# Scores' product with the keys' low parts over all 128 rows

## The chip, the cores and the metric

The kernel is one program on 1 core of one Trainium2 chip. The metric is the device time of one execution in microseconds (us). It is timed in several runs, and the median counts. Beside these runs stands one profiled execution, from which all rows below come. Line numbers with an L are those of the kernel before, unless the text says that they are of the changed kernel.

## The reference, cut to what matters

The whole computation has three stages: a recurrence over 768 tokens (4 batches, 8 heads), a feed-forward with a convolution, and an attention of four experts. The change is in the third:

```
for e in range(4):
    q = x @ wq[e]; k = x @ wk[e]; v = x @ wv[e]        # x: 4 x 768 x 320, heads of 64
    scores = (q @ k.T) / 8                             # causal
    a = softmax(scores)
    out += (gate of e, if e is among a token's best two) * (a @ v @ wo[e])
```

The inputs are float32, and the factor of 200 on `wq` and `wk` makes the scores large, so that the products are made from two parts of each operand: a high part in fp32r (what TensorE takes in one pass) and the rest, the low part, also in fp32r.

## The kernel before, in words

The recurrence and the feed-forward run side by side through the first 655 us. Then `setup_c` opens the tiles of the attention in the memory that the recurrence leaves, loads its weights through staging tiles `ws` (L637, tag "A", 6 buffers) and splits each into high and low part (L468 on ScalarE, L469 on VectorE). The last blocks of the feed-forward still run: their products are L551 and L574, their gates pass ScalarE at L468 (`gh`), L584 and L588, VectorE at L586, GpSimd at L469 (`gl`) and L589. From about 710 us only the attention is left.

`proj` makes queries, keys, values and gates of half of a batch. An expert has 64 dimensions, so that two experts share the 128 rows of a product. The tile `q` has, for expert e of a pair, the high parts of the queries in the 64 rows `Z[e]` and the low parts in the other 64. The tile `k` has the keys' high parts in both halves. The low parts of the keys stand in `kl`, two experts of a pair in one slot: expert 0 in rows 0 to 63, expert 1 in rows 64 to 127.

`weigh` then makes the scores of a block of 128 queries and one expert, for nk = 128 to 768 keys, in pieces (cuts) of at most 512 columns of PSUM. Each piece has two products: L748 multiplies all 128 rows of `q` with `k` (high and low queries times high keys), and L749 adds the high queries times the low keys, with the 64 rows of that expert alone. After the last piece of a block L751 adds the causal mask, in bf16. VectorE takes the maximum (L753), ScalarE the exponential (L755, into a tile `A`), GpSimd the scaling (L770), TensorE the transposes (L784), ScalarE and VectorE copy them (L789, L787), and TensorE weighs the values (L800) and multiplies with the output weights (L817). Copies of the result go through a tile `y` (L819, 2 buffers) to memory (L820). While the feed-forward still runs, tiles `A` come from the same 6 buffers as `ws`; afterwards from a larger pool.

Every matrix product in the program is a pair of instructions, a load of the stationary operand (PEld) and the product that streams the moving one (PE). The order on each engine is made by a scheduler when the program is built, from the code's order and from when it takes buffers to be free; on the chip each engine works its list in order.

Of the kernel before, what the change touches and what calls it, by code (L numbers as in the profile page):

```python
# [22 lines left out]
# the upper bits of the float64 that is float32's least normal, as a float32  # L23
# [7 lines left out]
def merge(streams, end=1e9):  # L31
    """Runs generators side by side: each yields how far along it is, and the one least far along goes on."""
    live = [[-9.0, k, g] for k, g in enumerate(streams)]
    while live:
        m = min(live)
        if m[0] > end:
            return
        try:
            m[0] = next(m[2])
        except StopIteration:  # L40
            live.remove(m)


def paced(g, start, span):
    """The progress that a generator yields as a share of its own, in the common time."""
    for f in g:
        yield start + span * f


class Kernel:  # L50
    """Heads of a tile are (b, hq, al, be), head = 4 hq + 2 al + be of batch b; a tile n holds 64
    tokens, two chunks of 32, of all batches. Columns of the tiles are u = (p, c), p = (b, hq)."""
# [4 lines left out]
    # ---------------------------------------------------------------- recurrence  # L57
    def setup_a(self, ctx):
        tc, nc = self.tc, self.nc
        cp = self.cp = ctx.enter_context(tc.tile_pool(name="acst", bufs=1))  # L60
        self.wk = ctx.enter_context(tc.tile_pool(name="awk", bufs=2))
        self.w = cp.tile([128, 32, 32], F32, name="w")
        self.kb = cp.tile([128, 16, 2, 2, 32], F32, name="kb")
        # rows of a head's a, then of the products of its tokens' a and k; beside them its state and values
        self.a = [cp.tile([128, 2, 2, 16, 32], F32, name=f"a{j}") for j in range(2)]
        self.SV = cp.tile([128, 2, 2, NP, 40], F32, name="SV")
        self.ra = cp.tile([128, NP, 2, 2, 32], F32, name="ra")
        # of each be the rows of its k and b and, in the other half, of its state; beside them what they are weighed with
        self.LB = [cp.tile([128, 2, NP, 2, 40], F32, name=f"LB{j}") for j in range(2)]
        self.RB = cp.tile([128, 2, NP, 2, 32], F32, name="RB")  # L70
        self.P = [cp.tile([128, 32, 32], F32, name=f"P{j}") for j in range(3)]
        # rows (p % 2, be, t)
        self.U = [cp.tile([128, NP // 2, 104], F32, name=f"U{j}") for j in range(2)]
        self.VZ = cp.tile([128, NP, 2, 2, 40], F32, name="VZ")
        self.VT = cp.tile([128, NP, 2, 64], F32, name="VT")
        self.sT = [cp.tile([128, NP, 104], F32, name=f"sT{j}") for j in range(2)]
        self.S = [cp.tile([128, NP, 2, 40], F32, name=f"S{j}") for j in range(2)]
        self.g21 = cp.tile([128, 8, 2, 16], F32, name="g21")
        self.d1 = cp.tile([128, 8, 32], F32, name="d1")
        self.M1 = cp.tile([128, 8, 2, 16], F32, name="M1")  # L80
        self.po = self.ps[3][:, 1].rearrange("p (a b) -> p a b", a=2)
        nc.vector.memset(self.w[32:64], 1.0)
        nc.gpsimd.memset(self.kb[32:64], 0.0)
        nc.gpsimd.memset(self.a[0][32:64], 0.0)
        nc.vector.memset(self.P[0][:, :, 0:1], 1.0)
        nc.vector.memset(self.po[:, 1], 0.0)
        nc.vector.memset(self.ps[1][:, 1, 256:], 0.0)
        cst = cp.tile([128, 164], F32, name="cst")
        self.ident, self.mask = cst[:, :128], cst[:, 128:160]
        self.m0, self.m1, self.m2 = cst[:, 160:161], cst[:, 161:162], cst[:, 162:163]  # L90
        self.cst = cst
        self.t = {}
        self.work = self.nn = 0
# [8 lines left out]
    def consts_b(self):  # L102
        """As consts_a(), what the first tile's preparation doesn't need."""
# [18 lines left out]
    def load_a(self, n):  # L122
        """Of each pair of heads side by side in the rows, the one's and the other's."""
# [9 lines left out]
    def load_v(self, k):  # L133
        """The values of a chunk, at the places that they are read from."""
# [10 lines left out]
    def load_ra(self, k):  # L145
        """Of each pair of heads side by side in the rows, the columns of one and of the other."""
# [13 lines left out]
    def mm(self, ns, *a, **k):  # L160
        """A product beside which the feed-forward runs, with what it takes of the tensor engine."""
# [7 lines left out]
    def prep(self, n):  # L169
# [4 lines left out]
        def early(tag, shape, name):  # L174
            """The second tile's come before the first one is done, and take room of the feed-forward."""
# [5 lines left out]
        for k in range(1, 5):  # L181
            x = early("xd", [128, 32, 16], "L1") if k == 1 else wk.tile([128, 32, 32 >> k], F32, name=f"L{k}", bufs=1)
            # not amid the solve of the tile before, that more waits for
# [30 lines left out]
        # of each head the products of the tokens' a with their k and with their b  # L214
# [20 lines left out]
        # the two halves' blocks of I + G, one to a lane (q, half, u), and the block below them  # L235
# [5 lines left out]
        # the first tile's solve goes before the weights' conversion: it holds the tiles of the latter  # L241
# [10 lines left out]
        # rows (half, t) of the blocks below, of heads u of the one half and u + 8 of the other  # L252
# [47 lines left out]
        # the blocks below, of two heads at a time, times those above their right; then times those above their left  # L300
# [98 lines left out]
    def post(self, k):  # L399
# [12 lines left out]
        def po(p0):  # L412
            """While there is no feed-forward the second half takes a bank of its."""
# [43 lines left out]
    # ---------------------------------------------------------------- convolved feed-forward  # L457
# [13 lines left out]
    def narrow(self, name, src, n):  # L471
        """float32 of a block of float64 weights, put together from their bits; magnitudes under
        float32's least normal give zero."""
# [33 lines left out]
    def ff(self):  # L507
        """The feed-forward of all tiles; the second product of a step of two blocks runs beside the
        first one of the next step."""
# [90 lines left out]
        k = 0  # L600
# [17 lines left out]
    # ---------------------------------------------------------------- expert attention  # L618
    def setup_c(self, ctx):
# [14 lines left out]
        for dst, nm, n, rows in ((self.wvg, "w_vg", 260, 3), (self.wqk, "w_qk", 512, 3), (self.wo, "w_o", DM, 2)):  # L634
            for k in range(rows):
                s = cw.tile([128, S], F32, tag="A", name="ws", bufs=6)[:, :n]
                nc.sync.dma_start(s, i[nm][k])  # L637
                self.split(dst[:, k, 0], dst[:, k, 1], s)
        self.c = [{} for _ in range(B)]
        self.lone = False  # L640
        self.apool, self.nA, self.nT = cw, 6, 2
        self.turns = dict.fromkeys("stmo", 0)

    def bank(self, kind):
        """Scores, transposes, the other products, the values' sums: each in turn in its banks of PSUM;
        there are fewer while the feed-forward still runs."""
# [10 lines left out]
    def proj(self, b, h):  # L657
        """Queries, keys, values and gates of half of a batch's tokens."""
# [5 lines left out]
        if h == 0:  # L664
            t["k"] = cw.tile([128, 4, S], F32R, name="k", bufs=2)
            t["kl"] = cw.tile([128, 2, S], F32R, name="kl", bufs=2)
# [6 lines left out]
        # high and low parts of rows 0..127, 128..255, and of the last 64 together  # L673
# [19 lines left out]
        # queries of an expert: the one half of the rows has the high, the other the low part; keys: both the high  # L693
        for m, z in ((0, 0), (2, 1), (1, 2), (3, 3)):
# [4 lines left out]
            for e in range(2):  # L699
                r, o = Z[e], Z[1 - e]  # L700
                hi, lo = (q[:, 2 * m + e], q[o, 2 * m + e]) if m < 2 else (k[:, 2 * m - 4 + e, cs], kl[r, m - 2, cs])
                if m < 2:
                    # the queries take the scores' scale, a power of two
# [29 lines left out]
    def weigh(self, b, i, pr):  # L733
        """The weighted attention of a block of queries, of a pair of experts."""
# [6 lines left out]
        for e in range(2):  # L741
            r = slice(64 * e, 64 * e + 64)
# [3 lines left out]
            for c0, c1 in zip(cuts, cuts[1:]):  # L746
                ce = 2 * pr + e
                nc.tensor.matmul(sp[:, c0:c1], q[:, ce, 128 * j:128 * j + 128], k[:, ce, c0:c1], start=True, stop=False)  # L748
                nc.tensor.matmul(sp[:, c0:c1], q[r, ce, 128 * j:128 * j + 128], kl[r, pr, c0:c1], start=False,  # L749
# [10 lines left out]
    def scale(self, b, i, pr):  # L760
        """The weights over their sums and times the gates."""
# [11 lines left out]
    def turn(self, b, i, pr):  # L773
        """The transposes of the weights."""
# [18 lines left out]
    def values(self, b, i, pr):  # L793
        """The values' sums by these weights."""
# [15 lines left out]
    def result(self, b, i, pr):  # L810
        """The product with the experts' output weights."""
        nc, cw = self.nc, self.cwk
        if pr:
# [4 lines left out]
            y = cw.tile([128, DM], F32, name="y")  # L818
# [4 lines left out]
    # ---------------------------------------------------------------- all of it  # L823
    def run(self):
        tc, nc = self.tc, self.nc
        with ExitStack() as top:
            self.dp = top.enter_context(tc.tile_pool(name="dram", bufs=1, space=DRAM))
            self.x2 = self.dp.tile([B, S, DM], F32, name="x2")
            # pairs of banks: recurrence; second product; first product, preparation; transposes, results
# [52 lines left out]
    def merge(self, streams, side):  # L882
        """Runs the streams by progress, and as much of the one beside them as the work of the tensor engine calls for."""
# [17 lines left out]
    def attention(self, ff, top, bctx):  # L901
        """The blocks of queries one after the other, the weights of the next beside the values of the
        last, the projections before they are needed, and the rest of the feed-forward at first."""
# [40 lines left out]
def layouts(inputs):  # L944
    """The inputs as the tiles read them: permuted, repeated or with rows left out, no arithmetic."""
# [3 lines left out]
    # axes of heads(): b hq al be n c t e  # L949
# [10 lines left out]
    def bits(x):  # L960
        """float64 as its raw bits; float32 as it is."""
        return x.view(np.int64) if x.dtype == np.float64 else x

    # rows of w_in: (al, hq, be, e < 32), then (hq, be, al, e >= 32) twice
# [45 lines left out]
```

## Time and profile before

| what | value |
|---|---|
| runs | 1004.41, 997.58 and 1007.2 us, median 1004.41 |
| profiled execution | span 1001.0 us from first to last instruction, 31990 instructions |
| PE / PEld busy | 814.1 us (81%) / 678.6 us (68%) |
| DVE / ACT / POOL busy | 741.2 (74%) / 585.6 (59%) / 510.2 (51%) us |
| mean granted TensorE clock | 0.908 of full speed |

The span is 3.4 us under the median of the runs and inside their spread of 9.6 us; the profiled execution's own device time is not listed apart from its span. Busy shares are means over stages of different kind; which engine sets the time is read stage by stage in the rows further down. Times of matrix products include the filling and emptying of the array, so that neighbouring products overlap in the listing: how long one holds the engine is the distance from its start to the next start.

### The profile page before, as it was taken

The page shows a single profiled execution, that of the slowest core. Times are in us where ns is not written, and L with a number is a line of the kernel's source. Part 1 is how long each engine was busy: PE and PEld are TensorE (multiplying, and loading weights), DVE is VectorE, ACT ScalarE, POOL GpSimd, SP SyncE. Part 2 cuts the span into 40 slices and gives each one's busy share as a digit, 9 for nine tenths or more (in the row PEclk, how much of TensorE's full clock was granted, in tenths as well). Part 3 has the DMA queues.
Part 4 walks back from the last instruction along what each step waited for, and adds up shares of the span by engine and source line. Part 5 has one row for each costly group of instructions (what it writes and reads, how often), then busy time and mean ns, then how long its engine had stood idle before and what let it go on. Part 6 is the DMA issues. An engine that isn't in the chain of part 4 may idle for free.

```text
span 1001.0 us, 31990 instructions
## 1 busy us (share of the span) xinstructions
PE 814.1 (81%) x13112; PEld 678.6 (68%) x13112; DVE 741.2 (74%) x1675; ACT 585.6 (59%) x1379; POOL 510.2 (51%) x614
## 2 busy tenths in 40 slices
PE   1365649968797878787778789859999999999998
PEld 1255548757686767667677678848777767777766
DVE  6887995988979898979888985546565646666544
ACT  0164648747575656565557577747566555655554
POOL 6455665655647465655656565654234333233342
PEclk9995569978889789978898999879999999999999
DMA  5345553635363535444344445141110100010000
GB/s 115 95 139 133 138 121 85 149 81 114 75 142 90 123 77 122 117 100 102 93 97 121 96 101 121 43 117 32 35 33 21 34 14 28 28 34 14 16 12 34
DMA packets 143491, 81.20 MB, mean 81 GB/s; under 512 B 113858, under 2 KB 127042, under 8 KB 142386
## 3 DMA queue, kind: packets, MB, share of 16 engines
q1 hardware_dynamic: 138450, 74.34, 30.5%
q0 software_dynamic: 4896, 4.83, 2.2%
q8 instruction: 103, 1.69, 0.7%
q14 instruction: 42, 0.34, 0.1%
HBM read 51.63 MB, written 11.80 MB: 63 GB/s over the span
## 4 chain that ended last, share of the span: by engine, by line
PE 43%; DVE 28%; DMA 10%; ACT 9%; issue 5%; POOL 2%; SPq 2%; DVEq 0%; ACTq 0%; POOLq 0%
PE ps L163 6%; PE ps L800 5%; PE ps L749 5%; PE ps L697 4%; DVE cv L586 4%; PE ps L784 4%; PE ps L551 4%; PE ps L748 3%; PE ps L574 3%; DMA xd<-xs 3%; DVE t L261 3%; DVE Q L200 3%; DMA xs<-xe 3%; DVE a L211 3%; PE ps L817 3%
## 5 line engine op out<-in xcount | busy, mean ns | idle before, releaser
L770 POOL TENSOR_TENSOR A<-A,rs 128x128 f32<-128x128 f32 (+5 forms) x96 | 87.7, 934 | 145.0 <-DVE rs L768 81.0
L586 DVE SCALAR_TENSOR_TENSOR cv<-h,cw,cv 128x256 f32<-128x256 f32 (+1 forms) x192 | 103.4, 567 | 34.2 <-ACT cv L584 32.7
L574 PE MATMUL ps<-wout,gh 128*128 128x320 f32 x384 | 94.4, 343 | 12.6 <-ACT gh L468 12.3
L551 PE MATMUL ps<-xh,win 128*128 128x256 f32 x384 | 93.5, 301 | 11.7 <-ACT xh L527 10.7
L430 POOL TENSOR_TENSOR RB<-RB,cst 64x256 f32<-64x256 f32 x96 | 79.5, 828 | 32.3 <-ACT RB L429 18.4
L753 DVE TENSOR_REDUCE nm<-ps 128x1 f32<-128x128 f32 (+5 forms) x96 | 59.8, 623 | 46.9 <-PE ps L751 36.9
L755 ACT ACTIVATE A<-ps,nm 128x128 f32<-128x128 f32 (+5 forms) x96 | 60.8, 634 | 55.5 <-DVE nm L753 42.5
L551 PE MATMUL ps<-xl,win 128*128 128x256 f32 x384 | 92.6, 296 | 0.1
L589 POOL TENSOR_TENSOR cv<-cv,h 128x512 f32<-128x512 f32 (+1 forms) x48 | 62.2, 1297 | 59.6 <-ACT cv L588 58.8
L469 POOL TENSOR_TENSOR gl<-cv,gh 128x512 fp32r<-128x512 f32 x48 | 63.2, 1316 | 34.9 <-ACT gh L468 33.2
L551 PEld LDWEIGHTS ps<-xh,win 128*128 128x128 f32 x384 | 70.8, 202 | 14.4 <-ACT xh L527 11.6
L261 DVE TENSOR_TENSOR t<-TT,G 128x1 f32<-128x1 f32 (+4 forms) x180 | 77.0, 428 | 4.7
L574 PEld LDWEIGHTS ps<-wout,gh 128*128 128x128 f32 x384 | 68.3, 208 | 15.5 <-ACT gh L468 13.6
L551 PEld LDWEIGHTS ps<-xl,win 128*128 128x128 f32 x384 | 69.8, 199 | 0.9 <-POOL xl L529 0.2
L163 PE MATMUL ps<-RB,LB 104*40 104x32 f32 (+1 forms) x1536 | 49.9, 217 | 25.0 <-DVE xe L445 15.7
L163 PEld LDWEIGHTS ps<-RB,LB 104*40 104x40 f32 (+1 forms) x1536 | 43.2, 133 | 32.7 <-issue 18.8
L163 PE MATMUL ps<-kb,a 40*32 40x64 f32 x1536 | 37.5, 257 | 33.9 <-DVE kb L207 23.9
L163 PE MATMUL ps<-VZ,KB 128*40 128x80 f32 x768 | 47.1, 288 | 21.6 <-ACT VZ L359 21.4
L574 PE MATMUL ps<-wout,gl 128*128 128x320 f32 x192 | 61.0, 347 | 1.8 <-POOL gl L469 1.8
L800 PE MATMUL ps<-AT,v 128*64 128x128 f32 x672 | 57.4, 286 | 0.3 <-DVE mx L726 0.3
L749 PE MATMUL ps<-kl,q 64*128 64x256 f32 (+3 forms) x144 | 57.6, 400 | 0.0
L163 PEld LDWEIGHTS ps<-VZ,KB 128*40 128x40 f32 x768 | 40.2, 152 | 25.7 <-ACT VZ L359 23.5
(176 smaller groups left out, 2302.4 us busy)
## 6 DMA issues: line engine op xcount, KB each, us to landing
kb<-in_kb_e_dram SPq DMA_DIRECT2D x24, 320.0 KB
LB<-KB SPq DMA_DIRECT2D x48, 160.0 KB
LB<-S SPq DMA_DIRECT2D x46, 100.0 KB
a<-in_a_e_dram SPq DMA_DIRECT2D x24, 160.0 KB
VT<-in_vt_dram SPq DMA_DIRECT2D x48, 80.0 KB
RB<-in_rb_dram SPq DMA_DIRECT2D x48, 80.0 KB
SV<-in_v_dram SPq DMA_DIRECT2D x48, 80.0 KB
VZ<-in_v_dram SPq DMA_DIRECT2D x96, 40.0 KB
```

Source lines behind the costliest of these rows:

```text
L163: self.nc.tensor.matmul(*a, **k)
L261: nc.vector.tensor_tensor(pr[:, :k, :k], TT[:, :k, :k], G[:, k:k + 1, :k].to_broadcast([128, k, k]), op=ALU.mult)
L430: nc.gpsimd.tensor_tensor(y, y, self.mask[s, None].to_broadcast([64, 8, 32]), op=ALU.mult)
L469: (eng or self.nc.vector).tensor_tensor(lo, x, hi.bitcast(F32), op=ALU.subtract)
L551: nc.tensor.matmul(hp[:, dd], wt[:, 128 * d:128 * d + 128], x, start=k == 0, stop=k == 7)
L574: nc.tensor.matmul(self.ps[1][:, tb, :DM], x, wt, start=d == 0 and k == 0, stop=d == 7 and k == 2)
L586: nc.vector.scalar_tensor_tensor(y, h[:, dd, :, k:k + nt], self.cw[:, k, d:d + 1], y, op0=ALU.mult, op1=ALU.add)
L589: (nc.gpsimd if GM and st % GM == 0 and st >= GN else nc.vector).tensor_tensor(cv[:, :, :, :nt], cv[:, :, :, :nt], h[:, :, :, 1:1 + nt], o ...
L749: nc.tensor.matmul(sp[:, c0:c1], q[r, ce, 128 * j:128 * j + 128], kl[r, pr, c0:c1], start=False, stop=c1 < nk)
L755: nc.scalar.activation(A[:, :nk], sp[:, :nk], AF.Exp, bias=nm, accum_out=sums[:, e:e + 1])
L770: nc.gpsimd.tensor_tensor(A[:, :nk], A[:, :nk], rs[:, e:e + 1].to_broadcast([128, nk]), op=ALU.mult)
L800: nc.tensor.matmul(op[64 * e:64 * e + 64], v[:, kt, 128 * pr + 64 * e:128 * pr + 64 * e + 64], ATs[kt][:, e], start=kt == 0, stop=kt == n ...
```

## The change

The keys' low parts move from a tile of two slots to one of four, a slot for each expert, like `k`. The 64 rows of the other expert in a slot hold zeros, written once on GpSimd. L749 then takes all 128 rows of `q` and of `kl`, and its stationary operand is the same as that of L748. The two `kl` tiles are made once in `setup_c` and used by batches in turn, where before they came from a pool with two buffers. The larger tiles take room: `ws` and the `A` tiles before the feed-forward has ended get 3 buffers where they had 6, and `y` gets 1 where it had 2. The change also takes comments out of the file, which moves line numbers by 4 or 5 in what follows.

```diff
@@ setup_c
-                s = cw.tile([128, S], F32, tag="A", name="ws", bufs=6)[:, :n]
+                s = cw.tile([128, S], F32, tag="A", name="ws", bufs=3)[:, :n]
                 nc.sync.dma_start(s, i[nm][k])
                 self.split(dst[:, k, 0], dst[:, k, 1], s)
+
+        self.kl = [cp.tile([128, 4, S], F32R, name=f"kl{j}") for j in range(2)]
+        for t in self.kl:
+            for e in range(2):
+                nc.gpsimd.memset(t[Z[1 - e], e::2].bitcast(F32), 0.0)
...
-        self.apool, self.nA, self.nT = cw, 6, 2
+        self.apool, self.nA, self.nT = cw, 3, 2
@@ proj
-            t["kl"] = cw.tile([128, 2, S], F32R, name="kl", bufs=2)
+            t["kl"] = self.kl[b % 2]
...
-                hi, lo = (q[:, 2 * m + e], q[o, 2 * m + e]) if m < 2 else (k[:, 2 * m - 4 + e, cs], kl[r, m - 2, cs])
+                hi, lo = (q[:, 2 * m + e], q[o, 2 * m + e]) if m < 2 else (k[:, 2 * m - 4 + e, cs], kl[r, 2 * m - 4 + e, cs])
@@ weigh
-            r = slice(64 * e, 64 * e + 64)
...
-                nc.tensor.matmul(sp[:, c0:c1], q[r, ce, 128 * j:128 * j + 128], kl[r, pr, c0:c1], start=False,
+                nc.tensor.matmul(sp[:, c0:c1], q[:, ce, 128 * j:128 * j + 128], kl[:, ce, c0:c1], start=False,
                                  stop=c1 < nk)
@@ result
-            y = cw.tile([128, DM], F32, name="y")
+            y = cw.tile([128, DM], F32, name="y", bufs=1)
```

Every engine keeps the same set of instructions, but for four zeroings on GpSimd and two more loads of a function table on ScalarE. Where they stand moves in the stage in which the attention's weights arrive. On ScalarE's list, from the splits of the weights on (`wvg`, `wqk`, `wo` are the weights, `x` the projections' input, `gh` a gate of the feed-forward, `xl` and `xh` its next input), there stood before:

```order
L468 ACTIVATE wvg<-ws 128x260 x3
L468 ACTIVATE wqk<-ws 128x512
L468 ACTIVATE gh<-cv 128x512
L468 ACTIVATE wqk<-ws 128x512 x2
L468 ACTIVATE wo<-ws 128x320 x2
L530 ACTIVATE xl<-xd 64x256
L527 ACTIVATE xh<-xd 128x768
```

and now:

```order
L468 ACTIVATE wvg<-ws 128x260 x3
L468 ACTIVATE wqk<-ws 128x512
L468 ACTIVATE x<-ps 128x2x128
L468 ACTIVATE wqk<-ws 128x512 x2
L468 ACTIVATE x<-ps 64x128
L468 ACTIVATE wo<-ws 128x320
L468 ACTIVATE gh<-cv 128x512
L468 ACTIVATE wo<-ws 128x320
```

The gate `gh` moved from behind the first split of `wqk` to behind the first split of `wo`, and a projection's first inputs moved ahead of it.

On the queue of SP, which issues the loads of the weights, one transfer moved (`xt` is a projection's input, `bef` a constant):

```order
 L633 DMA bef<-in_consts_dram 128x16
 L637 DMA ws<-in_w_vg_dram 128x260 x3
+L668 DMA xt<-x_57 128x3x320
 L637 DMA ws<-in_w_qk_dram 128x512 x3
 L637 DMA ws<-in_w_o_dram 128x320 x2
-L663 DMA xt<-x_57 128x3x320
```

The first load of `xt` now stands ahead of the weights `wqk` and `wo`.

On GpSimd's list at the same place (`cidb` and `negm` are constants, `h` a tile of the feed-forward):

```order
 L630 DMA cidb<-in_consts_dram 128x128
 L631 DMA negm<-in_consts_dram 128x128
+L643 MEMSET kl_9296 64x2x768 x2
+L643 MEMSET kl_9297 64x2x768 x2
 L559 COPY h<-hc_72 128x8x2
 L563 MEMSET h 128x8
```

The four zeroings stand ahead of the feed-forward's copies and of what follows them on that engine.

## Rows read from the trace of the kernel before

**Rows 1.** Stages: window, length, busy PE, PEld, DVE, ACT, POOL; clock; DMA; GB/s.

```profile
655.00:670.00 15.00, 4.19 (x20) 3.01 (x18) 6.66 (x10) 5.64 (x12) 7.89 (x13) 0.75 0.75 191
...
710.00:985.00 275.00, 273.13 (x1887) 201.67 (x1886) 167.95 (x499) 156.06 (x425) 98.66 (x117) 1.00 0.08 25
985.00:1001.00 16.00, 12.53 (x93) 8.41 (x92) 4.25 (x20) 7.88 (x25) 2.70 (x6) 0.98 0.11 41
```

**Rows 2.** Chain of waits from 707 to 1001 us, shares by line.

```profile
by line: PE ps L800 16.5%; PE ps L749 15.3%; PE ps L784 14.1%; PE ps L697 13.6%; PE ps L748 10.0%; PE ps L817 8.7%; PE ps L688 7.3%; PE ps L751 5.0%; PE ps L679 2.6%; DVE nm L753 1.1%; issue 0.9%; DVE mx L727 0.4%; PE ps L574 0.4%; ACT AT L
```

**Rows 3.** Timeline of TensorE's products: start us, duration us, instruction, count.

```profile
862.56 0.37 PE L688 MATMUL ps<-wvg,x 128*128 128x260 f32 x1
862.77 0.28 PE L748 MATMUL ps<-k,q 128*128 128x256 f32 x1
862.98 0.38 PE L749 MATMUL ps<-kl,q 64*128 64x256 f32 x1
863.29 0.23 PE L751 MATMUL ps<-negm,cidb 128*128 128x128 bf16 x1
863.33 0.83 PE L688 MATMUL ps<-wvg,x 128*128 128x260 f32 x5
```

**Rows 4.** Timeline of TensorE's loads of stationary operands, same stretch.

```profile
862.64 0.19 PEld L748 LDWEIGHTS ps<-k,q 128*128 128x128 f32 x1
862.97 0.18 PEld L749 LDWEIGHTS ps<-kl,q 64*128 64x128 f32 x1
```

**Rows 5.** Timeline of products around a piece of 512 keys.

```profile
758.95 0.28 PE L784 MATMUL ps<-cid,A 128*128 128x128 f32 x1
758.98 0.48 PE L748 MATMUL ps<-k,q 128*128 128x512 f32 x1
759.39 0.50 PE L749 MATMUL ps<-kl,q 64*128 64x512 f32 x1
759.82 0.23 PE L751 MATMUL ps<-negm,cidb 128*128 128x128 bf16 x1
759.89 0.93 PE L784 MATMUL ps<-cid,A 128*128 128x128 f32 x7
```

**Rows 6.** Chain of waits: start, length us, undisturbed rows of one line.

```profile
679.22 1.93 PE ps L551 x16
754.57 2.88 PE ps L697 x16
```

**Rows 7.** Line L749: duration ns min/median/max, first and last start, shapes.

```profile
L749 PE MATMUL ps<-kl,q x144: 322/381/502, 700.2 to 990.6; 64*128 64x256 f32 x64, 64*128 64x128 f32 x32, 64*128 64x512 f32 x32, 64*128 64x384 f32 x16
```

**Rows 8.** Waits from 707 us on: total us, times, longest us.

```profile
PEld ps L748 <- ACT A L755: 1.3, 4, 0.4
```

**Rows 9.** Groups of instructions: busy us, mean ns, idle before; a zeroing on POOL.

```profile
L106 POOL MEMSET SV<- 128x1280 f32 x1 | 1.2, 1160 | 0.0
```

**Rows 10.** Timeline of SP's queue: the weights' loads.

```profile
659.54 1.29 SPq L637 DMA_DIRECT2D ws<-in_w_vg_dram  x3
660.87 1.38 SPq L637 DMA_DIRECT2D ws<-in_w_qk_dram  x3
664.29 0.80 SPq L637 DMA_DIRECT2D ws<-in_w_o_dram  x2
```

**Rows 11.** Timeline of ScalarE; in brackets idle before and its releaser.

```profile
666.88 0.63 ACT L468 ACTIVATE wqk<-ws 128x512 fp32r<-128x512 f32 x1 [1.83 <-DMA ws<-in_w_qk_dram]
667.42 0.62 ACT L468 ACTIVATE gh<-cv 128x512 fp32r<-128x512 f32 x1
```

**Rows 12.** Timeline of TensorE at the same place.

```profile
668.09 1.44 PE L574 MATMUL ps<-wout,gh 128*128 128x320 f32 x4 [8.63 <-ACT gh L468]
```

**Rows 13.** Groups of instructions: a load of ScalarE's function table.

```profile
L588 ACT ACT_TABLE_LOAD x1 | 1.3, 1283 | 0.0
```

**Rows 14.** Timeline of the last two results: their transfers, the last copy.

```profile
996.28 2.31 SPq L820 DMA_DIRECT2D out_dram<-y  x2
997.79 0.44 ACT L819 ACTIVATE y<-ps 128x320 f32<-128x320 f32 x1 [1.03 <-PE ps L817]
```

## The prediction

> **What bounds the kernel now.** I read the stages first [rows 1]. From 710 to 985 us TensorE's products cover 273.13 of 275.00 us at full clock (1.00, the 2.4 GHz level), while VectorE has 167.95, ScalarE 156.06 and GpSimd 98.66. The reader is to see that one engine is full and no other near it: here a microsecond off TensorE's list is a microsecond off the time, until another engine's work comes too late. From 655 to 670 us it is the other way round: TensorE is busy for 4.19 of 15 us and the DMA share is 0.75; there latency sets the pace.
>
> The chain of waits then says which lines hold TensorE [rows 2]. Over the 294 us from 707 to 1001, L748 has 10.0%, L749 15.3% and the mask L751 5.0%: 29.4 + 45.0 + 14.7 = 89.1 us. L749 costs half as much again as L748, which has the same number of columns and twice the rows. The timeline shows why. Inside one list of products [rows 3], L748 starts 0.21 us behind an L688, L749 0.21 behind L748, L751 0.31 behind L749. The loads tell more [rows 4]: the load for L748 starts at 862.64, while the L688 that started at 862.56 runs, so it is hidden. The load for L749 starts only at 862.97, 0.01 us ahead of its own product, and takes 0.18 us in the open. A load for 64 rows behind a 128-row product is not started early, and the mask behind L749 pays once more (0.31 us for a product of 256 columns). What changes here between a hidden and an open load is the number of rows; type, columns and PSUM bank stay the same.
>
> **The change, part by part.**
>
> *The 144 low products* (64 of 256 columns, 32 of 128, 32 of 512, 16 of 384 [rows 7]) become 128-row products between 128-row products. I price them as the undisturbed rows of that form go: L551, 256 columns, 1.93 / 16 = 0.121 us; L697, 384 columns, 2.88 / 16 = 0.180 us [rows 6]; L784, 128 columns, (0.93 - 0.28) / 6 = 0.108 us [rows 5]; 512 columns, which no such row shows, by the same slope, 0.24 us (an estimate).
> - Group of 256 columns [rows 3]: 863.33 - 862.77 = 0.56 us, and the five L688 behind it take (0.83 - 0.28) / 4 = 0.1375 us each against 0.12, another 0.07: 0.63 us. Afterwards 2 x 0.121 + at most 0.108 for the mask = 0.35. Saved: 0.28 us.
> - Group of 512 columns [rows 5]: 759.89 - 758.95 = 0.94, less 0.108 for the L784 in it, 0.83 us. Afterwards 2 x 0.24 + 0.108 = 0.59. Saved: 0.24 us.
> - The same from the chain: 2 x (64 x 0.121 + 32 x 0.108 + 32 x 0.24 + 16 x 0.180) + 96 x 0.108 = 54 us against 89.1 us: 35 us, all of it in the full stretch.
>
> This is the lower end, since it lets the mask cost as much as an fp32 transpose. If it costs half (its bf16 load is hidden too), 96 x 0.054 = 5 us come on top, and 0.22 for 512 columns would give 1 more; if its neighbours also lose what they pay now behind it (0.07 x 96 = 7 us, which the chain books on them), 48 in all. I take **41 us**, between 35 and 48, nearer the lower end as the rows themselves give it.
>
> Against this stands a rule of the Trainium skill, "TensorE: Matmul & The Clock Gate", section "The mechanism" (of packing small matmuls): a load overlaps running products only where the row groups differ. By it a 128-row load never hides behind a 128-row product, the change would save nothing, and the time would stay near 1004 us and what the other parts add. The trace does not agree: in [rows 4] the 128-row load for L748 runs beside the 128-row L688 of [rows 3]. It stays as a rival below.
>
> *Waits that come up.* TensorE's list gets 41 us shorter in 275, the other engines' lists do not: VectorE goes from 61% to 168 / 234 = 72%, ScalarE to 67%. Neither is full, so no engine becomes the bound. But a score must pass VectorE, ScalarE and GpSimd before its transposes, and the two PSUM areas for scores must be free again. In all this stretch L748 waits 1.3 us for the exponential of an earlier score [rows 8], so there is slack, of unknown depth. Lower end 0, upper end half the gain, 20 us; I take **4 us**, nearer the row.
>
> *The arrival of the weights, 655 to 710 us.* Three things come later. (a) Four zeroings of 64 x 1536: by the row of 1280 elements, 1.16 us [rows 9], 1.39 us each, 5.6 us on GpSimd, ahead of the feed-forward's copies and the loads of its input. (b) With six buffers, `wqk` is issued right behind `wvg` at 660.87; with three it waits for the first split of `wvg`, as `wo` does now, to 664.29 [rows 10]: 3.4 us. The first split of `wqk` then moves from 666.88 to 670.3 [rows 11]. The gate `gh` now stands behind the first `wo`, whose transfer can only be issued after that split; how long it takes the trace does not show apart, and I take the 666.88 - 660.87 = 6.0 us of `wqk` as the upper price: `gh` at 670.3 + 0.6 + 6.0 = 676.9 at worst instead of 667.42. Behind `gh` on ScalarE stand `xl` and `xh`, the feed-forward's next input, and TensorE's L574. (c) Two more table loads of 1.28 us [rows 13], 2.6 us of ScalarE. The upper end is 9.5 + 2.6 = 12 us. The cover: TensorE idles 8.63 us there already [rows 12], and the projection's input `xt` moves ahead of `wqk`, so that its products, which had to be done anyway, fill part of the longer wait; at best this gains 2 us. With three `A` buffers a fourth exponential waits for the first transposes; it falls into the same time. From -2 to 12 I take **3 us**, since only the feed-forward's tail is late, not TensorE's other work. If the cover fails, it is the 12.
>
> *One buffer for `y`.* On average there are 11 us between results, far more than a transfer takes. Not so at the end: the last but one transfer is issued at 996.28, and the last copy starts at 997.79 [rows 14]. A transfer issued about 998.3 is what ends the span at 1001.0, so one takes some 2.5 us, and the last copy has to wait until about 998.8: **1 us**, at the very end with nothing to hide it.
>
> *Writing the low parts* into four slots instead of two costs nothing: the same instructions of the same size, hidden by TensorE. If that cover were gone, they would cost what they cost now.
>
> Sum: 1001.0 - 41 + 4 + 3 + 1 = 968.0 us of span. The median of the runs lies 3.4 us above the profiled span, so the forecast is **971 us**.
>
> **The rivals.**
> 1. *Waits eat the gain.* Scores come faster than VectorE and ScalarE hand them on; half of the 41 us turns into idle time of TensorE: 1004.4 - 20 + 4 = 988 us. For it: TensorE waits for nobody now, so nothing has tested how late the others are. Against it: their shares of 72% and 67%.
> 2. *Loads of equal rows do not overlap here* (the skill's rule). The low products then cost what they cost now: 0 saved, and the late weights and `y` remain: 1004.4 + 3 + 1 = 1008 us. [Rows 4] speak against it.
> 3. *Slower.* The same lost gain, and the chain of three buffers decides: `gh` goes out 9.5 us late, the table loads add 2.6, `y` 1: 1004.4 + 13 = 1017 us. It decides the sign only if the low products save less than 13 us, which is 0.09 us each, a third of the lowest value above.
>
> **How the numbers follow.** The forecast's case has 0.78, rival 1 has 0.12, rival 2 has 0.06, rival 3 has 0.04. The first case's own range goes from 1004.4 - 48 - 2 = 954 us (all of the gain, nothing lost) to 1004.4 - 35 + 8 + 3 = 980 us. To leave out no more than 2 in 10, the upper end goes on to rival 1, 989 us; the low end is 954 us. About 1% is what a measurement of this kernel can tell from no change. Faster by over 1% (under 994 us) are the first case and nearly all of rival 1: 0.90. Within 1% is rival 2 and a rest of rival 1: 0.07. Slower by over 1%, above 1014 us, is part of rivals 2 and 3: 0.03.
>
> **What would show it.** Loads of L749 that start while L748 runs, and L749 no dearer than L748 of the same columns. The share of the three lines in the chain falls from 89 us to 45 to 54. TensorE still near 100% in the middle of the attention; gaps there that end with the exponential, the transposes' copies or the scaling would be rival 1. Zeroings of some 1.4 us on GpSimd near 656 us; `gh` later than 667 us; the last feed-forward product a few us later. I am wrong if L749's load still starts when L748 ends, or if the attention's stretch shortens by much less than TensorE's list does.

## The result, and the profile after

The changed kernel takes **964.56 us** (median; 958.55 to 968.07, 4 runs) against 1001.77 us for the kernel before (997.58 to 1007.2, 4 runs): a ratio of 0.9627, 95% interval 0.9573 to 0.9681. The forecast was 971 us, faster. Times are 37.2 us apart; the forecast's drop was 1004.4 - 971 = 33.4. The measured time lies 6.4 us under the forecast: 3.8 us of that is the larger drop, and 2.6 us is that the median of before moved down from the one shown with the prediction.

The profiled execution of the changed kernel took 958.55 us, with a span of 956.8. Line numbers move: L697 of before is L702, L748 and L749 are L752 and L753, the mask L751 is L755, the exponential L755 is L759, L784 is L788, L800 is L804, L688 is L693, L817 is L821, L819 is L823. First the stages (window, length, busy PE, PEld, DVE, ACT, POOL; clock, DMA share, GB/s), to be set beside [rows 1]; the first of them starts at an event that is explained below, as that of [rows 1] does to within 0.2 us:

```profile
647.61:662.61 15.00, 5.10 (x20) 3.86 (x20) 6.71 (x10) 3.95 (x8) 12.07 (x15) 0.62 0.70 173
...
710.00:940.00 230.00, 224.96 (x1823) 184.47 (x1822) 161.75 (x483) 148.50 (x410) 97.25 (x115) 1.00 0.08 28
940.00:957.00 17.00, 13.02 (x104) 9.35 (x104) 5.32 (x22) 7.97 (x26) 3.75 (x8) 0.94 0.11 39
```

In the full stretch TensorE is a little less full: 5.04 us idle in 230, where before 1.87 were idle in 275. VectorE went from 61% to 70%. The ends of these windows were set by hand; how much shorter the attention became is counted in the table further down.

**Where to set the two traces side by side.** The two spans differ by 44.2 us, and not all of that is the change's. The last transfer that brings `xs`, the end of the recurrence that the change does not touch, is issued here and before at:

```profile
647.61 0.81 SPq L452 DMA_DIRECT2D xs<-xe  x1
```

```profile
655.18 0.81 SPq L452 DMA_DIRECT2D xs<-xe  x1
```

So 7.6 us were there ahead of anything that differs; over all nine profiles of this study this point lies between 645.7 and 655.2 us, without order. I call it the anchor. From it on I count, to the start of the last feed-forward product (708.26 us before, 703.97 after) and from there to the end of the span:

| kernel (one profile each) | `xs` to last feed-forward product | from there to the end | sum |
|---|---|---|---|
| before | 53.1 | 292.7 | 345.8 |
| changed | 56.4 | 252.8 | 309.2 |
| only the rows (below) | 52.6 | 256.6 | 309.2 |
| only the rooms (below) | 56.7 | 290.0 | 346.7 |
| buffers given back (below) | 51.2 | 255.2 | 306.5 |
| changed, once more (below) | 56.0 | 252.8 | 308.8 |
| low products side by side (below) | 52.1 | 288.2 | 340.2 |
| both products over 64 rows (below) | 51.8 | 285.9 | 337.7 |
| no low product (below) | 51.7 | 248.4 | 300.2 |

Behind the anchor the change is worth 36.6 us, as the medians say (37.2): the tail of the feed-forward comes 3.3 us later, the attention is 39.9 us shorter. The two profiles of the changed kernel differ by 0.4 us in this sum.

The shorter attention is in part earlier work. Behind the last feed-forward product stand, before, in the changed kernel and in the changed kernel with its buffers given back:

```profile
708.26:1001.00 292.74, 286.61 (x1983) 210.62 (x1981) 172.92 (x520) 165.29 (x451) 101.78 (x124) 1.00 0.08 26
```

```profile
703.97:956.80 252.83, 243.98 (x1969) 198.95 (x1967) 169.17 (x513) 159.57 (x445) 101.09 (x122) 1.00 0.09 30
```

```profile
697.46:952.70 255.24, 246.23 (x1983) 201.00 (x1981) 173.18 (x520) 162.24 (x451) 101.88 (x124) 1.00 0.09 30
```

The changed kernel has 14 products fewer there, because it did them ahead of the late feed-forward product: projections, their transposes and the scores of one more block.

The chain of waits from 707 us to the end (249.8 us), by line, beside [rows 2]:

```profile
by line: PE ps L804 18.3%; PE ps L788 15.3%; PE ps L702 14.5%; PE ps L821 9.2%; PE ps L752 9.1%; PE ps L693 7.9%; PE ps L753 7.4%; PE ps L684 2.5%; PE ps L755 2.4%; ACT A L759 2.4%; DVE nm L757 2.3%; issue 1.4%; DMA out_dram<-y 0.7%; DVE kl
```

High products, low products and mask: 9.1 + 7.4 + 2.4 = 18.9%, 47.2 us, where they had 89.1. The low products have become cheaper than the high ones. New are 2.4% (6 us) of ScalarE's exponential, and VectorE's maximum has gone from 1.1% (3.2 us) to 2.3% (5.7 us).

One list of products and its loads, where two pieces follow each other (start, duration), beside [rows 3 to 5]:

```profile
866.28 0.28 PE L752 MATMUL ps<-k,q 128*128 128x256 f32 x1
866.40 0.28 PE L753 MATMUL ps<-kl,q 128*128 128x256 f32 x1
866.52 0.39 PE L752 MATMUL ps<-k,q 128*128 128x512 f32 x1
866.75 0.40 PE L753 MATMUL ps<-kl,q 128*128 128x512 f32 x1
866.98 0.38 PE L788 MATMUL ps<-cid,A 128*128 128x128 f32 x2
```

```profile
866.11 0.19 PEld L752 LDWEIGHTS ps<-k,q 128*128 128x128 f32 x1
866.29 0.19 PEld L753 LDWEIGHTS ps<-kl,q 128*128 128x128 f32 x1
866.40 0.19 PEld L752 LDWEIGHTS ps<-k,q 128*128 128x128 f32 x1
866.52 0.19 PEld L753 LDWEIGHTS ps<-kl,q 128*128 128x128 f32 x1
```

Read the starts, not the durations: they are 0.12, 0.12, 0.23 and 0.23 us apart, where before the low product began 0.21 us behind a high one of 256 columns and the mask 0.31 behind that. Each load now begins while the product ahead of it runs (866.29 beside 866.28, 866.40 beside the low product of 866.40). The load of L753 brings the same columns of `q` as the load ahead of it, so one could think that this is why it is hidden; but the load of 866.11 brings other data than the projection L702 ahead of it, over the same 128 rows, and starts 0.17 us ahead of its own product too.

The mask behind a low product of 256 columns, and the mask's load:

```profile
717.50 0.28 PE L753 MATMUL ps<-kl,q 128*128 128x256 f32 x1
717.62 0.23 PE L755 MATMUL ps<-negm,cidb 128*128 128x128 bf16 x1
```

```profile
717.61 0.10 PEld L755 LDWEIGHTS <-cidb 128*128 128x128 bf16 x1
```

The mask's load starts 0.01 us ahead of the mask here too, as it does behind a 64-row product, so where it stands does not tell the two kernels apart. The distance from the low product to the mask does: 0.12 us, where it was 0.31. Per piece of 256 columns the change saves 0.21 - 0.12 = 0.09 us ahead of the low product and 0.31 - 0.12 = 0.19 behind it, 0.28 together.

All the low products have the new form, with a median of 281 ns where [rows 7] have 381:

```profile
L753 PE MATMUL ps<-kl,q x144: 271/281/401, 691.2 to 946.2; 128*128 128x256 f32 x64, 128*128 128x128 f32 x32, 128*128 128x512 f32 x32, 128*128 128x384 f32 x16
```

TensorE's waits from 700 us on (total, times, longest), products first, then loads, beside [rows 8]:

```profile
PE ps L752 <- ACT A L759: 3.1, 5, 1.1
PE ps L804 <- ACT AT L793: 0.7, 1, 0.7
```

```profile
PEld ps L752 <- ACT A L759: 4.9, 8, 1.3
PEld ps L804 <- ACT AT L793: 1.6, 4, 1.0
```

The two views count the same waits, once from the product and once from its load, so they are not added. The score's first product now waits for an earlier score's exponential, that is for its PSUM area: 3 to 5 us in all.

The arrival of the weights, 646 to 668 us: GpSimd, SP's queue, ScalarE and TensorE, beside [rows 9 to 13] (start, duration; in brackets idle before and what ended it).

```profile
649.07 5.62 POOL L643 MEMSET kl<- 64x1536 f32 x4
654.64 0.20 POOL L559 COPY h<-hc 128x16 f32<-128x16 f32 x1
```

```profile
651.96 1.28 SPq L637 DMA_DIRECT2D ws<-in_w_vg_dram  x3
653.29 0.43 SPq L668 DMA_DIRECT2D xt<-x  x1
655.15 3.57 SPq L637 DMA_DIRECT2D ws<-in_w_qk_dram  x3
659.75 0.33 SPq L637 DMA_DIRECT2D ws<-in_w_o_dram  x1
```

```profile
658.37 0.63 ACT L468 ACTIVATE wqk<-ws 128x512 fp32r<-128x512 f32 x1 [1.93 <-DMA ws<-in_w_qk_dram]
...
664.17 0.47 ACT L468 ACTIVATE wo<-ws 128x320 fp32r<-128x320 f32 x1 [0.29 <-DMA ws<-in_w_o_dram]
664.55 0.61 ACT L468 ACTIVATE gh<-cv 128x512 fp32r<-128x512 f32 x1
```

```profile
657.41 0.87 PE L684 MATMUL ps<-cid,xt 128*128 128x128 f32 x3 [8.26 <-DMA xt<-x]
```

Four zeroings take 5.62 us. `wqk` is issued behind the first split of `wvg`, 3.2 us after it in the queue where it was 1.3, and its three issues take 3.57 us where they took 1.38. Even so its first split is not late: it starts 658.37 - 647.61 = 10.8 us behind the anchor, 11.7 before (666.88 - 655.18). What is late is `wo`, 5.8 us behind that split, and `gh` behind it: `gh` starts 664.55 - 647.61 = 16.9 us behind the anchor, 12.2 before (667.42 - 655.18), so 4.7 us late. TensorE's long idle time ends with `xt` instead of `gh`, and other work of the attention comes ahead of `gh`. In the 15 us behind the anchor this makes little of a difference: TensorE is busy for 5.10 us (the first window above), and for 4.01 in the same 15 us before.

The last two results, beside [rows 14]:

```profile
951.28 0.44 ACT L823 ACTIVATE y<-ps 128x320 f32<-128x320 f32 x1 [0.24 <-PE ps L821]
953.62 0.44 ACT L823 ACTIVATE y<-ps 128x320 f32<-128x320 f32 x1 [1.42 <-DMA out_dram<-y]
```

ScalarE idles 1.42 us ahead of the last copy, which waits for the one buffer; before it idled 1.03 us there for the last product.

### The profile page after: what moved, and what is told of

It reads as the page before. It is cut to its first block, busy times and chain, and to the rows that moved or that the text cites. A ratio compares the mean times of both kernels' runs of the same rounds, so it can differ in the third digit from the quotient of the medians.

```text
span 956.8 us, 31993 instructions
## 1 busy us (share of the span) xinstructions
PE 771.2 (81%) x13112; PEld 664.9 (69%) x13112; DVE 737.1 (77%) x1675; ACT 584.8 (61%) x1381; POOL 517.1 (54%) x618
## 4 chain that ended last, share of the span: by engine, by line
PE 38%; DVE 29%; DMA 12%; ACT 10%; issue 5%; POOL 4%; SPq 3%; DVEq 0%; ACTq 0%; POOLq 0%
PE ps L163 6%; PE ps L804 5%; PE ps L788 4%; DVE cv L586 4%; PE ps L702 4%; DVE Q L200 3%; PE ps L551 3%; PE ps L574 3%; DMA xd<-xs 3%; DMA xs<-xe 3%; DVE t L261 3%; PE ps L693 3%; PE ps L821 2%; PE ps L752 2%; DVE L L186 2%
## 5 line engine op out<-in xcount | busy, mean ns | idle before, releaser
L759 ACT ACTIVATE A<-ps,nm 128x128 f32<-128x128 f32 (+5 forms) x96 | 60.9, 635 | 43.1 <-DVE nm L757 28.4
L469 POOL TENSOR_TENSOR gl<-cv,gh 128x512 fp32r<-128x512 f32 x48 | 65.6, 1366 | 34.4 <-ACT gh L468 33.0
L163 PE MATMUL ps<-RB,LB 104*40 104x32 f32 (+1 forms) x1536 | 51.7, 220 | 20.7 <-DVE xe L445 14.1
L163 PE MATMUL ps<-kb,a 40*32 40x64 f32 x1536 | 35.2, 248 | 31.7 <-DVE kb L207 23.0
L804 PE MATMUL ps<-AT,v 128*64 128x128 f32 x672 | 57.0, 286 | 0.7 <-ACT AT L793 0.7
L788 PE MATMUL ps<-cid,A 128*128 128x128 f32 x336 | 54.4, 279 | 0.4 <-POOL A L774 0.4
```

The costliest lines, as they stand in the source:

```text
L163: self.nc.tensor.matmul(*a, **k)
L469: (eng or self.nc.vector).tensor_tensor(lo, x, hi.bitcast(F32), op=ALU.subtract)
L759: nc.scalar.activation(A[:, :nk], sp[:, :nk], AF.Exp, bias=nm, accum_out=sums[:, e:e + 1])
L788: nc.tensor.transpose(tp[:, m, e], As[e][:, 128 * (2 * g + m):128 * (2 * g + m) + 128], self.cid)
L804: nc.tensor.matmul(op[64 * e:64 * e + 64], v[:, kt, 128 * pr + 64 * e:128 * pr + 64 * e + 64], ATs[kt][:, e], start=kt == 0, stop=kt == n ...
```

## The experiments

The theory: the gain is the load of a 64-row product, which stands open between 128-row products; what was given up to make room for the four-expert tile (the rooms: buffers, and time on GpSimd for the zeros) costs a few us of it. Against it stood four other ways to read the result: fewer rows changed nothing and the rearranged buffers gave the gain; 64 rows are dear in themselves; the loss of buffers costs much more than it seems; and the gain is bounded by other engines already. All ratios are to the kernel before on the same chip.

**Only the rows** (the kernel before, with its buffers; the low product runs over both experts' rows of the two-expert tile, so the queries' low parts meet the other expert's low keys, which the reference has not).

```
- matmul(sp[:, c0:c1], q[r, ce, ...], kl[r, pr, c0:c1], start=False,
+ matmul(sp[:, c0:c1], q[:, ce, ...], kl[:, pr, c0:c1], start=False,
```

> The kernel before with one edit: L749 multiplies all 128 rows, on the old two-slot tile, so that the queries' low parts meet the other expert's low keys (small wrong terms in the scores). Buffers and zeroings stay as before. Theory (a change of the number of rows between neighbouring products keeps a load from hiding): all of the attention's gain and none of the costs, 1002 - 41 = 961 us, 957 to 967, ratio about 0.96; L749's loads start while L748 runs, and from the last feed-forward product to the end 292.7 us become about 251. Rival (the gain comes from the other order of the lists and the other buffers): 1002 us.

Measured: 963.32 us against 997.68, ratio 0.9651 (0.9591 to 0.9712). Two operands of one line, cut to other rows, give a gain that is not told apart from that of the whole change, without a column less or a buffer moved. The stretch behind the last feed-forward product went from 292.7 to 256.6 us; the expected 251 had left out the waits that come up, for which the forecast had 4 us. Its chain from 707 us on (251 us):

```profile
by line: PE ps L800 18.7%; PE ps L697 15.3%; PE ps L784 15.1%; PE ps L817 9.4%; PE ps L748 9.1%; PE ps L688 7.8%; PE ps L749 7.5%; DVE nm L753 2.8%; PE ps L679 2.8%; PE ps L751 2.4%; ACT A L755 2.2%; issue 1.3%; ACT AT L789 0.8%; ACT k L468
```

The three lines have 19.0%, 47.7 us, as in the changed kernel, and the exponential and the maximum have come up just as far. So the new waits belong to the shorter products, not to the smaller pools.

**Only the rooms** (the changed kernel with its four-expert tile, zeroings and pools, but a 64-row low product).

```
- matmul(sp[:, c0:c1], q[:, ce, ...], kl[:, ce, c0:c1], start=False,
+ matmul(sp[:, c0:c1], q[64*e:64*e+64, ce, ...], kl[64*e:64*e+64, ce, c0:c1], start=False,
```

> The changed kernel with L749 back on 64 rows: four slots, zeroings, 3 and 1 buffers stay. Theory: only the costs are left, 1002 + 3.3 (from the end of the recurrence to the last feed-forward product) + 1.2 (last copy waits for y) = 1006 us, 1002 to 1011. Rival (order and buffers made the gain): about 965 us.

Measured: 1001.01 us against 997.68, ratio 1.0047 (1.0014 to 1.0081), which is 4.7 us more (1.4 to 8.1); the expected 1006 had started from 1002. With the old product the rooms cost about what the two terms of the forecast (3 + 1) say. The row that the rival with the long chain of buffers hung on, `gh`, comes here as in the changed kernel:

```profile
668.35 0.61 ACT L468 ACTIVATE gh<-cv 128x512 fp32r<-128x512 f32 x1
```

That is 668.35 - 651.45 = 16.9 us behind the anchor.

**The low products side by side** (the kernel before; of a block of scores first the high products of all its pieces, then the low ones, each over 64 rows).

```
- for c0, c1 in pieces: high(c0, c1); low(c0, c1)
+ for c0, c1 in pieces: high(c0, c1)
+ for c0, c1 in pieces: low(c0, c1)
```

> The kernel before, but in a block of two pieces both high products go first and both 64-row products after them. Theory (each change of rows and back costs 0.3 us): 48 blocks have one such round instead of two, 48 x 0.29 = 14 us less, 988 us, 983 to 993; the second low product's load starts while the first runs. Rival (every load for 64 rows is slow in itself, whatever stands before it): 1002 us and an open load at every low product.

Measured: 996.3 us against 997.68, ratio 0.9973 (0.9942 to 1.0003): not told apart from no change, and the size expected is excluded. In the kernel's list of instructions the scheduler kept only 12 of the 48 blocks with two pieces in that order; in 18 it put other products between, in the other 18 the next high one. By the 0.29 us that I had expected of each, 12 make 3.5 us, which the interval holds. (Behind the anchor its one profile is 5.6 us shorter, which it just holds too.) So the experiment did not do what it was to do, and its time tells little. What it shows is one of the 12, products and then loads:

```profile
759.56 0.39 PE L748 MATMUL ps<-k,q 128*128 128x256 f32 x2
759.89 0.50 PE L750 MATMUL ps<-kl,q 64*128 64x256 f32 x2
760.32 0.23 PE L752 MATMUL ps<-negm,cidb 128*128 128x128 bf16 x1
```

```profile
759.88 0.29 PEld L750 LDWEIGHTS ps<-kl,q 64*128 64x128 f32 x2
760.31 0.10 PEld L752 LDWEIGHTS <-cidb 128*128 128x128 bf16 x1
```

Two low products take 760.32 - 759.89 = 0.43 us, where one in [rows 3] takes 0.31 until the mask starts. Both loads are over in 0.29 us, so the second began while the first product ran. The second product adds 0.43 - 0.31 = 0.12 us, what one of 256 columns takes between equal rows.

**Both products over 64 rows** (the kernel before; the high product leaves out the queries' low parts).

```
- matmul(sp[:, c0:c1], q[:, ce, ...], k[:, ce, c0:c1], start=True, stop=False)
+ matmul(sp[:, c0:c1], q[r, ce, ...], k[r, ce, c0:c1], start=True, stop=False)
```

> The kernel before with L748 on 64 rows too, which leaves out the queries' low parts times the high keys. Theory (change of rows): L749's load hides behind L748, now of equal rows; L748's own load is open where 128 rows stand before it; 48 rounds fewer, about 988 us. Rival (loads for 64 rows are slow in themselves): both lines open at every product, 144 x 0.1 to 0.2 us more than before, 1016 to 1030 us.

Measured, in a single run: 989.83 us against 997.68, below every run of before in that comparison (991.8 to 1003.31). Twice as many 64-row products, and no time lost, which rules out the rival's 1016 us and more. The drop is 7.9 us, where the expectation had 14 (1002 to 988). In the trace TensorE goes 122 times from 128 rows to 64, where before it went 144 times and not 48 times less; at 0.28 us each the 22 make 6.2 us. One piece, products and loads:

```profile
757.58 0.38 PE L748 MATMUL ps<-k,q 64*128 64x256 f32 x1
757.80 0.28 PE L749 MATMUL ps<-kl,q 64*128 64x256 f32 x1
758.01 0.23 PE L751 MATMUL ps<-negm,cidb 128*128 128x128 bf16 x1
```

```profile
757.58 0.18 PEld L748 LDWEIGHTS ps<-k,q 64*128 64x128 f32 x1
757.69 0.19 PEld L749 LDWEIGHTS ps<-kl,q 64*128 64x128 f32 x1
758.01 0.10 PEld L751 LDWEIGHTS <-cidb 128*128 128x128 bf16 x1
```

The load of L749 has the same 64 rows and now starts at 757.69, 0.11 us into the product of L748: hidden. The open one is that of L748, which comes behind 128 rows; and the mask comes 0.21 us behind a product of 256 columns, not 0.12 as between equal rows. It is the **change** of rows that costs, in either direction. This is what the forecast read from [rows 4]. There are two limits. By the kernels' code, the 64-row loads that are hidden here and in the experiment before this one bring the same columns of `q` as the load ahead of them; a hidden one with other data in the same 64 rows is shown nowhere. And the time holds something else besides, as these rows of the same kernel show:

```profile
804.13 0.50 PE L748 MATMUL ps<-k,q 64*128 64x256 f32 x2
804.35 0.52 PE L749 MATMUL ps<-kl,q 64*128 64x256 f32 x2
```

```profile
804.13 0.19 PEld L748 LDWEIGHTS ps<-k,q 64*128 64x128 f32 x2 [0.17 <-issue]
```

Two loads are over in 0.19 us, where one takes 0.18, and two products, one of 256 and one of 512 columns, are followed by the next after 0.22 us. They run side by side, which 16 pairs of L748 in this trace do; no 128-row products of these lines do so. How much of the 7.9 us this gives was not tried apart.

**The buffers given back** (the changed kernel; the weights of the first two tables staged in two tiles that lie idle then, six buffers for `wo` and for the first scores, two for `y`; the zeroings stay).

```
+ st = cw.tile([128, 6, 256], F32, tag="v", name="wsv", bufs=2)   # wvg, wqk
- s = cw.tile([128, S], F32, tag="A", name="ws", bufs=3)[:, :n]
+ s = st[:, 512*k:512*k+n] if rows == 3 else cw.tile([128, DM], F32, tag="A", name="ws", bufs=6)
- A = self.apool.tile([128, S], F32, tag="A", ..., bufs=3)
+ A = self.apool.tile([128, S if self.lone else DM], F32, tag="A", ..., bufs=6)
- y = cw.tile([128, DM], F32, name="y", bufs=1)
+ y = cw.tile([128, DM], F32, name="y", bufs=2)
```

> The changed kernel with its buffers back: wvg and wqk are staged in the two tiles that the values take later, so that all loads can be issued at once; wo and the A tiles of the feed-forward's time have 6 buffers of 320 columns, y has 2. The zeroings on GpSimd stay. Theory (the lost buffers cost 3 us at the weights' arrival and 1.2 us at the end): 4 us under the changed kernel run beside it; the last copy no longer waits for the transfer before it, and from the end of the recurrence to the last feed-forward product it is 53 to 54 us as before the change, not 56.4. Rival (the late feed-forward only trades places with projections, which then need not be done later): 1 us under it, that of y alone.

**The changed kernel once more**, beside it on the same chip:

> The changed kernel once more, as the measure beside the one before it: ratio 0.963, 0.957 to 0.968.

Measured: 958.05 us (0.9610, 0.9584 to 0.9635) with the buffers back, 956.69 us (0.9620, 0.9573 to 0.9667) for the changed kernel. The gain repeats, and the two are not told apart by their times, so that neither the expected 4 us nor the rival's 1 us is decided by them. Behind the anchor the profile with the buffers back is 2.3 to 2.7 us shorter (306.5 against 308.8 and 309.2), one profile against two. It also shows why it is not 4. The last copy no longer waits for a transfer, as expected. The gate is back where it was before the change,

```profile
658.38 0.61 ACT L468 ACTIVATE gh<-cv 128x512 fp32r<-128x512 f32 x1
```

658.38 - 646.23 = 12.2 us behind the anchor, and the last feed-forward product comes 51.2 us behind it (expected: 53 to 54), not 56.0 to 56.4. Since the zeroings stay in this kernel, it is the buffers and not the zeroings that make it late. But the stretch from there to the end grows from 252.8 to 255.2: the 14 products that TensorE had run during the wait stand behind it again (1983 products there, not 1969).

**No low product at all** (the kernel before without L749; the high queries never meet the keys' low parts).

```
- matmul(sp[:, c0:c1], q[r, ce, ...], kl[r, pr, c0:c1], start=False, stop=c1 < nk)
```

> The kernel before without L749; the high queries times the low keys are left out of the scores. Theory (TensorE is still the bound after the change): beyond the 35 us of the kernel with rows alone, the low products' own 19 us go too (7.5% of 250 us in its chain), of which the growing waits take a few: 945 us, 940 to 950. Rival (VectorE and ScalarE set the time by now): 955 us or more, with gaps on TensorE that end with the exponential.

Measured: 951.72 us against 996.8, ratio 0.9544 (0.9513 to 0.9574). Against the kernel with the rows alone, which ran on another chip, the ratio is 0.0107 lower, some 10 us, and behind the anchor the profile is 309.2 - 300.2 = 9.0 us shorter; the work left out holds 7.5% of 251, 19 us, of that kernel's chain. Neither side of the expectation had it: about half. Full stretch, longest wait of TensorE's loads, and chain:

```profile
710.00:930.00 220.00, 210.90 (x1664) 170.38 (x1663) 155.73 (x469) 144.74 (x402) 94.09 (x110) 0.99 0.09 29
```

```profile
PEld ps L747 <- ACT A L752: 5.2, 10, 1.8
```

```profile
by line: PE ps L797 16.5%; PE ps L781 12.6%; PE ps L697 12.5%; PE ps L814 8.9%; PE ps L688 8.7%; PE ps L747 7.5%; DVE nm L750 6.8%; ACT A L752 5.5%; PE ps L679 2.7%; issue 2.5%; PE ps L748 1.7%; DVE kl L469 1.3%; ACT AT L786 1.2%; DVE rs L7
```

TensorE is idle for 9.1 of 220 us; the exponential is the longest of its waits there, but several other engines' results hold it up as well. The maximum and the exponential hold 12.3% of the chain, where they have 4.7% in the changed kernel. The forecast's first rival, waits that eat half of the gain, is what the next step would meet.

## Why the prediction held, step by step

- **The low products, 41 us.** The chain's share fell by 89.1 - 47.2 = 41.9 us, and the kernel that changes the rows alone has the same sum behind the anchor as the whole change, 309.2 us. The terms by piece hold too: 256 columns at 0.12 us and 512 at 0.23 (0.121 and 0.24 were taken). In the group of 256 columns two sizes were off and cancel: the mask holds TensorE for 0.04 to 0.07 us and not 0.108 (717.62 to the next product at 717.68), but the products behind it still pay the 0.07 that the sum counted as saved: in the changed kernel seven projections behind a mask, from 730.11 us on, take (1.08 - 0.28) / 6 = 0.133 us each against 0.12, which is 0.08 in all.
- **Loads of equal rows that don't overlap, rival 2.** The Trainium skill, "TensorE: Matmul & The Clock Gate", section "The mechanism", says in its list of what overlaps that a load overlaps running products only where the row groups differ. The trace does not agree, before or after: the load of 866.29 has the rows of the product that started at 866.28 and runs beside it. In the kernel with both products over 64 rows it is the load with equal rows that is hidden. An earlier paragraph of the same section also lets a load into the background weight buffer be pulled ahead; the rival was built on the list alone. The hidden loads of equal rows fit that paragraph; that a load of other rows stands open between them follows from neither.
- **New waits, 4 us.** TensorE's idle time in the full stretch is 5.04 us of 230, where before the same length would have had 1.6 (1.87 x 230 / 275): 3.4 us more, and most of it ends with the exponential (3.1 us of the products' waits), as the sketch of rival 1 had it.
- **The weights' arrival, 3 us.** The last feed-forward product is 3.3 us later behind the anchor, `gh` 4.7 (9.5 was the upper price). Of the two steps in that price one did not come: the first split of `wqk` was to be 3.4 us later and is 0.9 earlier behind the anchor; the other, `wo` behind that split, took 5.8 us (6.0). The zeroings took 5.62 us (5.6), the function tables are loaded five times from 640 to 720 us, three before. The time was right to within what can be told, but it is not all lost: 14 products of the attention went into the gap, and when the buffers were given back, 2.4 us came back at the other end. In the changed kernel, then, the rooms cost between nothing (its sum behind the anchor, 309.2 us, is that of the kernel with the rows alone) and the 4.7 us measured with the old products; that stays open, at about the scatter of the runs.
- **One buffer for `y`, 1 us.** This term was too large. The last copy starts 0.79 us behind the last product (953.62 against 952.83), where before it started 0.39 behind it: the one buffer costs 0.4 us.
- **What was off.** The drop was 37.2 us, not 33.4. By the rows, -41.9 + 3.4 + 3.3 + 0.4 gives -34.8 where the profiles have -36.6 behind the anchor. The excess of 1.8 us has the sign and about the size of the 14 products that are done early (2.4 us, when they were put back), whose gain the forecast allowed only as an end of its range. That the forecast still came this near has some luck in it, since the terms for `y` and for the weights were each off by a little and the 41 us were chosen between 35 and 48. Against the medians nothing more can be said: the interval of the ratio is 32 to 43 us of gain, and the forecast's 33.4 lies in it.

## What to carry to other kernels

On a full TensorE look at the distance from start to start and at the rows of the loads, not at durations or counts of columns: a product that differs in rows from its neighbours pays on both sides, here 0.09 us ahead of it and 0.19 until the next. If there is room, fill it up with zeros to its neighbours' rows, or put such products next to each other, and look whether the scheduler leaves them there. Before two profiles are compared, find an event that the change can't have moved, and count from there.

## What the hardware showed unexpectedly

- Two 64-row products with the same queries, next to each other, pay for the change of rows once: in the kernel with both over 64 rows the load ahead of the pair is open (0.18 us), the second is hidden, and the pair takes 758.01 - 757.58 = 0.43 us to the mask, the same as the two adjacent low products of the third experiment. A single low product takes 0.31 [rows 3]. What costs time is going from 128 rows to 64 and back.
- With TensorE still 98% busy (224.96 of 230 us), another 19 us taken off its list were worth only some 10 us, and 9.1 us of 220 turned up as idle time of TensorE: so near to full, the busy share did not tell how close the scores' way over VectorE and ScalarE had come.
- A stretch that the change does not touch ended anywhere from 645.7 to 655.2 us in the nine profiles. These 9.5 us are as large as all side terms of the forecast together.
